# First six attention steps of a fused attention and expert kernel: own-token bonus summed on TensorE, second copy of V made on ScalarE and VectorE, new due dates for the planner

## The chip, the cores and the metric

One core of one Trainium2 chip runs the whole program. The metric is the device time of one execution in microseconds (us); of the kernel before, three timed runs are shown and one further execution that was profiled.

## The reference

The input goes through three layers. The first is a linear attention with a decaying state per head (4 sequences, 8 heads, 768 tokens, 48 values per head), in which each token also sees its own key and value through a bonus vector `u`. The second is a feed-forward layer of 384 by 2048 with a softplus. The third sends each of the 3072 tokens to one of 8 experts of 384 by 1024, by a greedy choice under a capacity of 384 tokens per expert.

```python
for t in range(S):
    cur = np.einsum('bhd,bhe->bhde', u[None] * kt, vt)
    y[:, :, t] = np.einsum('bhd,bhde->bhe', rt, state + cur)
    state = w[None, :, :, None] * state + np.einsum('bhd,bhe->bhde', kt, vt)
...
h = x @ w_in
g = np.maximum(h, 0.0) + np.log1p(np.exp(-np.abs(h)))
x = g @ w_out
...
out[mask] = np.maximum(x[mask] @ w1[e], 0.0) @ w2[e]
```

The bonus of one token and head is therefore a single number, the sum over d of r times u times k, times that token's V.

## The kernel before

**Work and stages.** Tokens go in 24 attention steps of 128 (64 tokens of two sequences) and in 8 blocks of 384 (three steps each). A step loads K, R and V (`kn`, `rn`, `vn`, two buffers each, six DMAs on SP's queue, L367) and V a second time in another layout into the lower or upper rows of `X` (two DMAs, L373), whose other rows hold the running state. VectorE scales K and R by powers of the decay (`ks`, `rs`), TensorE transposes both (L466 and L470), the results are copied to `kT` and `ar` (L351 on ScalarE, L353 on VectorE), TensorE multiplies them (`prods`, L491), VectorE masks the products (L499), TensorE forms the state's addition (`fresh`, L520) and the step's output (`outs`, L553). VectorE makes the bonus by itself: R times K (`rk`), that times `ut`, a reduction over d to `sd` (L543), and V times `sd` to `sv`, which L558 adds to the output as it leaves its bank. In the first block `tx` (L566) transposes the result into `xt`.

**Feed-forward.** Block 0 multiplies in float32: `w_in` by L673 and `w_out` by L785. Both weights arrive as 64-bit floats, in 16 chunks each (L607 and L624, four raw buffers in `third`), and VectorE makes 32-bit floats of each chunk with three instructions (L599, L601, L603). Each `w_out` chunk is also transposed (L633) and multiplied with the gate (L637). Later blocks use weights split into two 16-bit halves, which VectorE and ScalarE make (L617 and L649 the lower halves), in L678 and L788 to L790. After that come the choice of experts and the experts, which the change leaves as they are.

**What sets the order.** The program is not written in the order in which it runs. Each `op(...)` is an item with an engine, a duration, the keys it reads and writes and a due date, and `lay_out` builds every engine's list by a simulation of its own: the engine that can start first takes, among its items that could start within SLACK of each other, the one with the earliest due date. An item that names two engines goes where it would be taken first. Banks of PSUM are handed out in the same pass, and one `sp` list holds all of SP's DMAs. Once built, each engine runs its list strictly in that order and waits where something is not ready. Where TensorE's list has a gap in the simulation, `keep_warm` (L143) puts in products of a zero tile with itself, called fills below; a change to or from items marked `small` counts as a gap (SWITCH), so it gets one fill as well. Due dates come from T0, LEN and the other constants at L251 to L287: `due_att(n)` for step n, OUTLATE as a delay of the outputs from step 6 on, AHEAD as a lead of the steps over the feed-forward.

Of the kernel before, what the change touches and what calls it, by code (L numbers as in the profile page):

```python
# [9 lines left out]
FT = mybir.dt.float32  # L10
HF = mybir.dt.float16
# [3 lines left out]
OP = mybir.AluOpType  # L15
AX = mybir.AxisListType
# [5 lines left out]
def tile_kernel(ctx, tc, r, k, v, w, u, w_in, w_out, w_gate, w1, w2, out):  # L22
    nc = tc.nc
    B, H, S, D = r.shape
    DM, F = w_in.shape
# [225 lines left out]
    T0 = 15500.0  # L251
# [22 lines left out]
    AHEAD = 7500.0  # L274

    TURNED, TURN = 6, 1500.0
    HALFL = 4000.0
    HALFL2 = -4000.0
    NLAT = 6
    LATL = 400.0  # L280
    OUTLATE = 5000.0
    RAWL = 17600.0
    BITL = 14000.0
    SPLITL = -3900.0
    WOUTL = 6100.0
    ATT0 = 2600.0
    LOADL = 1600.0  # L287
# [4 lines left out]
    def several(pool, n, shape, dtype, name):  # L292
        return [pool.tile(shape, dtype, name=f"{name}{i}") for i in range(n)]
# [14 lines left out]
    XHL = several(work, 2, [128, 2 * DM], HF, "xhl")  # L308
# [30 lines left out]
    def product(o, a, b, r, w, due):  # L339
        op("dve", 470.0, lambda: DVE.tensor_mul(o, a, b), r=r, w=w, due=due)  # L340


    def scaled(eng, o, a, by):
        if eng == "act":
            ACT.mul(o, a, by)  # L345
        else:
            DVE.tensor_scalar(o, a, by, None, op0=OP.mult)

    def copied(eng, o, a):
        if eng == "act":  # L350
            ACT.copy(o, a)  # L351
        else:
            DVE.tensor_copy(o, a)  # L353
# [6 lines left out]
    def load_step(n):  # L360
        GROUP[0] = "att"
        b0, s0 = step_tok(n)
        i = n % 2
        due = due_att(n) - LOADL
        for key, src, store in (("kn", k, KN), ("rn", r, RN), ("vn", v, VN)):
            for b in range(2):
                op("sp", 650.0, lambda b=b, src=src, store=store: SP.dma_start(  # L367
                    store[i][b * 64:(b + 1) * 64], src[b0 + b, :, s0:s0 + C, :].rearrange("h s d -> s h d")),
                    w=[(key, i, b)], due=due, size=546.0)
        for q in range(2):  # L370
            src = bass.AP(tensor=v.tensor, offset=v.offset + ((b0 * H + q) * S + s0) * D,
                          ap=[[D, C], [2 * S * D, 2 * HP], [1, D]])
            op("sp", 650.0, lambda q=q, src=src: SP.dma_start(  # L373
                X[n % 3][(1 - q) * 64:(2 - q) * 64, q].rearrange("p b a d -> p (b a) d"), src),
                w=[("xv", n % 3, q)], due=due + 3.0, size=546.0)
# [15 lines left out]
                              for q in range(2)], w=["wt"], due=-1e9, size=168.0)  # L391
    op("sp", 450.0, lambda: SP.dma_start(
        ut, bass.AP(tensor=u.tensor, offset=u.offset, ap=[[0, 128], [1, H * D]])), w=["ut"], due=-500.0, size=546.0)
# [29 lines left out]

    op("dve", 3200.0, powers, r=["wt"], w=["pw", ("ar", 1, 0)], due=-1e8)
# [19 lines left out]
    def attention(n):  # L444
# [94 lines left out]


        product(rk, RN[i], KN[i], rnk + knk, ["rk"], due + 3)
        product(rk, rk, ut.rearrange("p (h d) -> p h d", h=H), ["ut"], ["rk"], due + 3)
        op("dve", 470.0, lambda: DVE.tensor_reduce(sd, rk, axis=AX.X, op=OP.add), r=["rk"], w=[("sd", i)], due=due + 3)  # L543
        product(sv, VN[i], sd[:, :, None].to_broadcast([128, H, D]), vnk + [("sd", i)], [("sv", i)], due + 3)
# [36 lines left out]
        else:  # L581
            xh, xl = XHL[i][:, :DM], XHL[i][:, DM:]
            op(FROM_SBUF, 0.0, lambda eng: scaled(eng, xh, xf, 64.0), r=[("xf", i)], w=[("xhl", i, 0)], due=due + 5)
# [9 lines left out]
    def from_double(src, t, key, due):  # L593
# [3 lines left out]
        op("sp", 450.0, lambda: src(raw), w=[("raw", c % 4)], due=due - RAWL, size=1092.0)  # L597
# [23 lines left out]
    def prep_wout(f):  # L621
# [19 lines left out]
        op("pe", 330.0, mm, r=[wt, "gate"], due=due, bank=b2)  # L641
# [751 lines left out]
    total = lay_out(items, lambda it: (it.prio, it.n), {}, True)  # L1393
# [25 lines left out]
```

## Time and profile before

| what | us |
|---|---|
| median of three runs | 778.96 (777.51 to 786.61) |
| the profiled execution's own time | 775.64 |
| its span in the trace | 773.9 |
| TensorE / VectorE / ScalarE busy in the span | 749.8 / 624.9 / 404.1 |

The span runs from the first to the last instruction; 1.74 us of the execution lie outside it. The granted TensorE clock is given as a share of the full clock (mean 0.996). TensorE's matmuls overlap in the trace, so that the time from one start to the next, not the duration, tells what one costs. A fill counts as busy.

### The profile page before, as it was taken

To read this page: it belongs to the slowest core of one execution; us is meant where nothing else is said; L and a number is where in the kernel's file an instruction comes from. 1 tells how busy PE (TensorE), PEld (TensorE's weight loads), DVE (VectorE), ACT (ScalarE), POOL (GpSimd) and SP (SyncE) were. 2 spreads that over 40 slices of the span, in tenths; PEclk is the share of its full clock that TensorE was granted. 3 is DMA by queue.
4 is the path that set the end of the run, shared out by engine and by line. 5 is a ranking of instruction groups with operands and counts; after the bars stand their busy time and mean duration, and the time that the engine had idled before them with its cause. 6 is when DMAs were issued, how large, how long until landed. Compare 5 with 4: busy or idle time off the path is not lost.

```text
span 773.9 us, 18327 instructions
## 1 busy us (share of the span) xinstructions
PE 749.8 (97%) x7202; PEld 493.0 (64%) x7202; DVE 624.9 (81%) x1711; ACT 404.1 (52%) x808; POOL 81.2 (10%) x109
## 2 busy tenths in 40 slices
PE   7999999999999999999999999999999999998996
PEld 6865677666566666667676666666666665655663
DVE  7898998999998787788999977887789879877420
ACT  2165533799766666567889911211145424436731
POOL 1000000000000000000001000000232131317731
PEclk9999999999999999999999999999999999999999
DMA  7887764412343233333110003441385664837700
GB/s 137 172 183 191 211 171 77 83 22 62 69 91 66 56 68 62 62 67 71 36 22 11 2 12 94 118 121 50 97 208 165 174 175 143 211 108 191 216 31 30
DMA packets 170901, 80.04 MB, mean 103 GB/s; under 512 B 136512, under 2 KB 166464, under 8 KB 170816
## 3 DMA queue, kind: packets, MB, share of 16 engines
q1 hardware_dynamic: 167744, 69.44, 38.3%
q0 software_dynamic: 3072, 9.44, 4.0%
q8 instruction: 56, 0.92, 0.5%
q14 instruction: 29, 0.24, 0.1%
HBM read 61.55 MB, written 9.63 MB: 92 GB/s over the span
## 4 chain that ended last, share of the span: by engine, by line
PE 67%; DVE 18%; issue 4%; ACT 4%; DMA 4%; SPq 1%; POOL 1%; POOLq 0%; ACTq 0%; DVEq 0%
PE bank L678 14%; PE bank L1292 7%; PE bank L788 7%; PE bank L789 6%; PE bank L790 6%; PE bank L785 3%; PE bank L1310 3%; PE bank L1312 3%; PE bank L1311 3%; PE bank L553 2%; PE bank L673 2%; DVE ar L499 2%; DVE gf L691 2%; PE bank L1036 2%; DMA mraw<-moe_w 1%
## 5 line engine op out<-in xcount | busy, mean ns | idle before, releaser
L678 PEld LDWEIGHTS <-wi 128*128 128x128 f16 x1008 | 97.3, 98 | 65.2 <-issue 2.0
L678 PE MATMUL bank<-xt,wi 128*128 128x384 f16 x672 | 127.6, 326 | 0.0
L684 ACT ACTIVATE ta<-bank 128x384 f32<-128x384 f32 x128 | 61.5, 482 | 43.3 <-PE bank L678 30.2
L789 PE MATMUL bank<-wo,g 128*128 128x384 f16 (+1 forms) x240 | 78.4, 327 | 0.9 <-DVE wo L649 0.7
L788 PE MATMUL bank<-wo,g 128*128 128x384 f16 (+1 forms) x240 | 78.5, 327 | 0.0
L790 PE MATMUL bank<-wo,g 128*128 128x384 f16 (+1 forms) x240 | 78.5, 327 | 0.0
L691 DVE SCALAR_TENSOR_TENSOR gf<-bank,ta 128x384 f32<-128x384 f32 x112 | 61.8, 553 | 17.2 <-ACT ta L686 16.0
L678 PE MATMUL bank<-xs,wi 128*128 128x384 f16 x336 | 72.9, 326 | 0.0
L1292 PE MATMUL bank<-g,w1h 128*128 128x384 f16 x384 | 72.9, 326 | 0.0
L685 ACT ACTIVATE ta<-ta 128x384 f32<-128x384 f32 x128 | 66.5, 522 | 2.9
L686 ACT ACTIVATE ta<-ta 128x384 f32<-128x384 f32 x128 | 66.2, 519 | 2.5
L1312 PE MATMUL bank<-w2h,g 128*128 128x384 f16 x192 | 62.6, 326 | 0.0
L1310 PE MATMUL bank<-w2h,g 128*128 128x384 f16 x192 | 62.6, 326 | 0.0
L1311 PE MATMUL bank<-w2l,g 128*128 128x384 f16 x192 | 62.5, 326 | 0.0
L1296 ACT ACTIVATE g<-bank 128x384 f16<-128x384 f32 x64 | 30.7, 489 | 40.4 <-PE bank L1292 24.7
L1292 PEld LDWEIGHTS <-w1h 128*128 128x128 f16 x384 | 35.8, 98 | 22.6 <-issue 0.4
L1299 DVE SCALAR_TENSOR_TENSOR g<-bank,g 128x384 f16<-128x384 f32 x64 | 34.1, 548 | 19.4 <-ACT g L1296 19.3
L698 DVE SCALAR_TENSOR_TENSOR g<-gf,g 128x384 f16<-128x384 f32 x80 | 44.0, 553 | 3.1 <-ACT g L345 1.8
L499 DVE TENSOR_TENSOR ar<-bank,mask 64x256 f32<-64x256 f32 x96 | 40.5, 422 | 4.6 <-PE bank L491 2.3
L345 ACT ACTIVATE x2o<-bank 128x384 f16<-128x384 f32 x19 | 9.3, 490 | 65.3 <-PE bank L790 39.2
L1205 POOL DMA_INDIRECT third<-x2d,idx x24 | 25.8, 1074 | 155.7 <-DVE db L1009 130.0
L1292 PE MATMUL bank<-g,w1l 128*128 128x384 f16 x192 | 41.7, 326 | 0.0
(227 smaller groups left out, 1533.3 us busy)
## 6 DMA issues: line engine op xcount, KB each, us to landing
mraw<-moe_w SPq DMA_DIRECT2D x64, 384.0 KB, 4.0
third<-moe_w_in SPq DMA_DIRECT2D x16, 384.0 KB, 5.0
third<-moe_w_out SPq DMA_DIRECT2D x16, 384.0 KB, 3.5
kn<-k SPq DMA_DIRECT2D x48, 96.0 KB, 3.1
rn<-r SPq DMA_DIRECT2D x48, 96.0 KB, 3.1
vn<-v SPq DMA_DIRECT2D x48, 96.0 KB, 3.0
X<-v SPq DMA_DIRECT2D x48, 96.0 KB, 3.1
x2d<-x2o SPq DMA_DIRECT2D x48, 96.0 KB, 2.2
```

The costliest lines, as they stand in the source:

```text
L678: PE.matmul(ph, WF[:, f, a, kk, :], x[:, kk, :], start=(i == 0), stop=(i == 3 * KC - 1))
L684: op("act", 371.0, lambda: ACT.activation(ta, bank.view(BT), AF.Abs), w=[("ta", c)], due=due, bank=bank)
L685: op("act", 413.0, lambda: ACT.activation(ta, ta, AF.Exp, scale=-1.0), w=[("ta", c)], due=due)
L686: op("act", 413.0, lambda: ACT.activation(ta, ta, AF.Ln, bias=1.0), w=[("ta", c)], due=due)
L691: op("dve", 470.0, lambda: DVE.scalar_tensor_tensor(gf, bank.view(BT), 0.0, ta, op0=OP.max, op1=OP.add), r=[("ta", c)], w=[("gf", c)], due ...
L788: PE.matmul(p, gh[:, f, ts], WU[:, f, 0, :no], start=(f == 0), stop=False)
L789: PE.matmul(p, gh[:, f, ts], WU[:, f, 1, :no], start=False, stop=False)
L790: PE.matmul(p, gl[:, f, ts], WU[:, f, 0, :no], start=False, stop=(f == FC - 1))
L1292: PE.matmul(ph, a[:, kk, fs], XH[p][:, x0 + kk, :], start=(i == 0), stop=(i == 3 * KC - 1))
L1310: PE.matmul(po, h1h[:, f, js], w2h[:, fz, :], start=(f == 0), stop=False)
L1311: PE.matmul(po, h1h[:, f, js], w2l[:, fz, :], start=False, stop=False)
L1312: PE.matmul(po, h1l[:, f, js], w2h[:, fz, :], start=False, stop=(f == FB - 1))
```

## The change

For the first six steps the bonus is made in another way: VectorE multiplies the transposed R, still in its bank, with `kT` (one product of 128 by 512, called `rkT`, which lies in the memory of `xhl`), TensorE multiplies each head pair's part of it with a table `uw` of two columns that holds u times the decay (`sums`, four float32 matmuls of two columns), and VectorE multiplies V with these sums from their bank. `uw` comes from `uq`, two further small DMAs. The second copy of V is made in the first six steps from `vn`, in four copies of 64 by 192 by ScalarE or VectorE, in place of the two DMAs; V itself and everything from step 6 on stay. Several constants of due dates, DMA sizes and one duration of the planner are new, and the simulation's clocks of SP and VectorE start at 1000 and 900.

```diff
-    T0 = 15500.0
+    T0 = 16250.0
...
-    AHEAD = 7500.0
+    AHEAD = 10500.0
...
+    COPIED = 6
...
-    OUTLATE = 5000.0
+    OUTLATE = 8750.0
...
-    XHL = several(work, 2, [128, 2 * DM], HF, "xhl")
+    XHL2 = work.tile([128, 2, 2 * DM], HF, name="xhl")
+    XHL = [XHL2[:, i] for i in range(2)]
...
+        if n < COPIED:
+            for q in range(2):
+                for b in range(2):
+                    op({"act": 260.0, "dve": 180.0}, 0.0, lambda eng, q=q, b=b: copied(
+                        eng, X[n % 3][(1 - q) * 64:(2 - q) * 64, q, b],
+                        VN[i][b * 64:(b + 1) * 64].rearrange("p (a q) d -> p a q d", q=2)[:, :, q, :]),
+                        r=[("vn", i, b)], w=[("xv", n % 3, q)], due=due_att(n) + 2.5)
+            return
...
+    op("sp", 1300.0, lambda: [SP.dma_start(uq[q * 64:q * 64 + D], u.rearrange("(p q) d -> q d p", q=2)[q])
+                              for q in range(2)], w=["uq"], due=-1000.0, size=168.0)
     op("sp", 450.0, lambda: SP.dma_start(
-        ut, bass.AP(tensor=u.tensor, offset=u.offset, ap=[[0, 128], [1, H * D]])), w=["ut"], due=-500.0, size=546.0)
+        ut, bass.AP(tensor=u.tensor, offset=u.offset, ap=[[0, 128], [1, H * D]])), w=["ut"], due=due_att(3), size=1200.0)
...
+    def factors():
+        DVE.memset(uw, 0.0)
+        for q in range(2):
+            DVE.tensor_mul(uw[q * 64:q * 64 + D, :, q], uq[q * 64:q * 64 + D], wt[q * 64:q * 64 + D])
+
+    op("dve", 300.0, factors, r=["wt", "uq"], w=["uw"], due=2.5)
...
+        if n < TURNED:
+            op("dve", 602.0, lambda: DVE.tensor_tensor(rkT, b2.view(HP, 128), kT, op=OP.mult), r=[("kT", i)], w=["rkT"],
+               due=due + 3, bank=b2)
+
+            def sums():
+                for pr in range(HP):
+                    PE.matmul(b7.view(H)[:, 2 * pr:2 * pr + 2], rkT[:, pr, :], uw[:, pr, :], start=True, stop=True)
+
+            b7 = Bank("att")
+            op("pe", 900.0, sums, r=["rkT", "uw"], w=[("sd", i)], due=due + 3, bank=b7)
+            op("dve", 470.0, lambda: DVE.tensor_tensor(sv, VN[i], b7.view(H)[:, :, None].to_broadcast([128, H, D]), op=OP.mult),
+               r=vnk, w=[("sv", i)], due=due + 3, bank=b7)
+        else:
+            bonus()
...
-        op("pe", 330.0, mm, r=[wt, "gate"], due=due, bank=b2)
+        op("pe", 670.0, mm, r=[wt, "gate"], due=due, bank=b2)
...
-    total = lay_out(items, lambda it: (it.prio, it.n), {}, True)
+    total = lay_out(items, lambda it: (it.prio, it.n), {"sp": 1000.0, "dve": 900.0}, True)
```

The first place is the head of SP's list. In the kernel before, a chunk of `w_in`, the second copy of V (`X0`), `ut` and another chunk stand ahead of step 1's K (`kn1`):

```order
L390 DMA wt_139<-w 48x4x1 x2
L607 DMA third_131<-moe_w_in 128x3x256
L367 DMA kn0_93<-k 64x8x48 x2
L367 DMA rn0_91<-r 64x8x48 x2
L367 DMA vn0_95<-v 64x8x48 x2
L373 DMA X0_97<-v 64x8x48 x2
L392 DMA ut_140<-u 128x384
L607 DMA third_131<-moe_w_in 128x3x256
L367 DMA kn1_94<-k 64x8x48 x2
```

In the change it reads (`uq` is the small table of u):

```order
L400 DMA wt_138<-w 48x4x1 x2
L369 DMA kn0_93<-k 64x8x48 x2
L369 DMA rn0_91<-r 64x8x48 x2
L369 DMA vn0_95<-v 64x8x48 x2
L369 DMA kn1_94<-k 64x8x48 x2
L369 DMA rn1_92<-r 64x8x48 x2
L369 DMA vn1_96<-v 64x8x48 x2
L646 DMA third_130<-moe_w_in 128x3x256
L402 DMA uq_149<-u 48x4x1 x2
```

Five transfers that stood ahead of step 1's K are gone from there: two of `w_in`, two of `X0` and `ut`.

The second place is VectorE's list in step 2 (the third), from R times K on, in the kernel before:

```order
L340 TENSOR_TENSOR rk0_104<-rn0_91,kn0_93 128x384
L599 TENSOR_SCALAR wi_134<-third_131 128x384
L340 TENSOR_TENSOR rk0_104<-rk0_104,ut_140 128x384
L353 COPY ar0_111<-bank5_85 64x8x64
L527 TENSOR_TENSOR wx0_113<-bank6_86,wx0_113 128x4x48
L527 TENSOR_TENSOR wx0_113<-bank1_81,wx0_113 128x4x48
L543 TENSOR_REDUCE sd0_105<-rk0_104 128x8
L499 TENSOR_TENSOR ar0_111<-bank0_80,mask_144 64x4x64 x2
L499 TENSOR_TENSOR ar0_111<-bank2_82,mask_144 64x4x64 x2
L340 TENSOR_TENSOR wx0_113<-wx0_113,sq_145 128x384
L340 TENSOR_TENSOR sv0_107<-vn0_95,sd0_105 128x384
```

The same step in the change, from the copy to `ar` on:

```order
L355 COPY ar0_111<-bank5_85 64x8x64
L571 TENSOR_TENSOR xhl_116<-bank5_85,kT0_109 128x512
L640 SCALAR_TENSOR_TENSOR wi_133<-third_130,wi_133 128x384
L355 COPY X2_99<-vn0_95 64x192
L522 TENSOR_TENSOR ar0_111<-bank0_80,mask_143 64x4x64 x2
L355 COPY X2_99<-vn0_95 64x192
L522 TENSOR_TENSOR ar0_111<-bank1_81,mask_143 64x4x64 x2
L550 TENSOR_TENSOR wx0_113<-bank6_86,wx0_113 128x4x48
L550 TENSOR_TENSOR wx0_113<-bank4_84,wx0_113 128x4x48
L580 TENSOR_TENSOR sv0_107<-vn0_95,bank3_83 128x384
L342 TENSOR_TENSOR wx0_113<-wx0_113,sq_144 128x384
```

Two products and the reduction have become one product of 512 columns, and two of the four copies of V stand on VectorE here (the other two on ScalarE).

The third place is TensorE's list in a late block (the outputs of step 12). Before, `outs` stands by itself, behind a fill of its own and ahead of the feed-forward's next products:

```order
L790 MATMUL bank_82<-wo,g_130 128x392
L143 LDWEIGHTS still
L143 MATMUL bank_87<-still 128x128
L553 MATMUL bank_84<-X_97,ar_111 64x48 x16
L788 LDWEIGHTS g_129
L788 MATMUL bank_82<-wo,g_129 128x392
```

In the change it stands behind the next step's transposes, and its own step's `fresh` (L543, 16 matmuls of which the first is shown) and the next step's `prods` follow on it:

```order
L829 MATMUL bank_86<-wo,g_129 128x392
L489 MATMUL bank_85<-identf,ks_103 128x128 x4
L493 MATMUL bank_84<-identf,rs_101 128x128 x4
L143 LDWEIGHTS still
L143 MATMUL bank_87<-still 128x128
L592 MATMUL bank_81<-X_97,ar_111 64x48 x16
L543 MATMUL bank_82<-vn_95,ks_102 64x48
```

The outputs have moved back beside the next step's products, and one fill serves the three groups of small products.

## Rows read from the trace of the kernel before

**Rows 1.** Busy time by stretch: stretch, length, each engine's busy time, clock, DMA
```profile
6.58:37.83 31.25, 26.95 (x517) 23.70 (x517) 25.52 (x59) 7.06 (x13) 0.00 (x0) 0.95 0.83 167
...
39.00:86.06 47.06, 44.81 (x355) 28.93 (x356) 44.03 (x104) 26.71 (x56) 0.00 (x0) 1.00 0.79 193
86.06:142.10 56.04, 56.04 (x698) 40.89 (x698) 51.07 (x120) 22.96 (x57) 0.00 (x0) 1.00 0.60 137
142.10:173.80 31.70, 31.41 (x226) 19.03 (x225) 31.17 (x76) 29.37 (x70) 0.82 (x2) 1.00 0.22 42
```

**Rows 2.** The chain of waits in order of time: start us, us, what
```profile
39.00 4.14 PE bank L673 x12
44.82 1.95 PE bank L673 x6
55.73 3.95 DMA third<-moe_w_in
...
81.36 1.50 PE bank L637 x12
...
203.01 1.46 PE bank L678 x9
...
210.02 1.07 PE bank L553 x32
```

**Rows 3.** Timeline of VectorE before 38 us: start, us, instruction, idle before
```profile
12.56 0.56 DVE L340 TENSOR_TENSOR rk<-rk,ut 128x384 f32<-128x384 f32 x1 [1.85 <-DMA ut<-u]
...
16.59 0.56 DVE L340 TENSOR_TENSOR ks<-kn,pwn 128x384 f32<-128x384 f32 x1 [1.26 <-DMA kn<-k]
...
30.66 0.55 DVE L340 TENSOR_TENSOR rk<-rn,kn 128x384 f32<-128x384 f32 x1
31.13 0.35 DVE L599 TENSOR_SCALAR wi<-third 128x384 int32<-128x384 int32 x1
31.40 0.55 DVE L340 TENSOR_TENSOR rk<-rk,ut 128x384 f32<-128x384 f32 x1
32.17 0.69 DVE L353 COPY ar<-bank 64x512 f32<-64x512 f32 x1 [0.23 <-ACT ar L351]
...
33.44 0.54 DVE L543 TENSOR_REDUCE sd<-rk 128x8 f32<-128x384 f32 x1
...
36.30 0.55 DVE L340 TENSOR_TENSOR sv<-vn,sd 128x384 f32<-128x384 f32 x1
36.88 0.36 DVE L353 COPY X<-wx 64x384 f32<-64x384 f32 x1
37.27 0.56 DVE L558 TENSOR_TENSOR xf<-bank,sv 128x384 f32<-128x384 f32 x1
```

**Rows 4.** Timeline of SP's queue: start, us to issue, what
```profile
6.60 1.31 SPq L373 DMA_DIRECT2D X<-v  x2
7.96 0.62 SPq L392 DMA_DIRECT2D ut<-u  x1
...
9.10 1.29 SPq L367 DMA_DIRECT2D kn<-k  x2
```

**Rows 5.** Timeline of TensorE in the first block and in a late one
```profile
62.46 0.66 PE L466 MATMUL bank<-identf,ks 128*128 128x128 f32 x4 [1.56 <-DVE ks L340]
...
275.14 0.60 PE L466 MATMUL bank<-identf,ks 128*128 128x128 f32 x4
275.57 0.60 PE L470 MATMUL bank<-identf,rs 128*128 128x128 f32 x4
...
278.47 0.22 PE L143 MATMUL bank<-still 128*128 128x128 bf16 x1
278.62 0.69 PE L491 MATMUL bank<-ar,kT 64*64 64x64 f32 x32
279.13 0.63 PE L520 MATMUL bank<-vn,ks 64*64 64x48 f32 x32
279.70 0.34 PE L788 MATMUL bank<-wo,third 128*128 128x392 f16 x1
```

More of the change, by code (lines that the diff above doesn't have):

```diff
@@ L368, in load_step @@
                     store[i][b * 64:(b + 1) * 64], src[b0 + b, :, s0:s0 + C, :].rearrange("h s d -> s h d")),
-                    w=[(key, i, b)], due=due, size=546.0)
+                    w=[(key, i, b)], due=due, size=640.0)
+        if n < COPIED:
[6 more added lines that the diff above has]
+            return
         for q in range(2):
@@ L374, in load_step @@
                 X[n % 3][(1 - q) * 64:(2 - q) * 64, q].rearrange("p b a d -> p (b a) d"), src),
-                w=[("xv", n % 3, q)], due=due + 3.0, size=546.0)
+                w=[("xv", n % 3, q)], due=due + 3.0, size=640.0)
     wt = const.tile([128, HP], FT, name="wt")
@@ L538, in attention, with bonus @@
                    r=[("wx", 0), ("wx", 1)], w=[("st", y, q)], due=due + 3)
[L541 to L544, printed above, removed]
+        def bonus():
+            product(rk, RN[i], KN[i], rnk + knk, ["rk"], due + 3)
+            product(rk, rk, ut.rearrange("p (h d) -> p h d", h=H), ["ut"], ["rk"], due + 3)
+            op("dve", 470.0, lambda: DVE.tensor_reduce(sd, rk, axis=AX.X, op=OP.add), r=["rk"], w=[("sd", i)], due=due + 3)
+            product(sv, VN[i], sd[:, :, None].to_broadcast([128, H, D]), vnk + [("sd", i)], [("sv", i)], due + 3)
+        if n < TURNED:
[10 more added lines that the diff above has]
+            bonus()
         b5, b6 = Bank("att"), Bank("att")
@@ L582, in attention @@
             xh, xl = XHL[i][:, :DM], XHL[i][:, DM:]
-            op(FROM_SBUF, 0.0, lambda eng: scaled(eng, xh, xf, 64.0), r=[("xf", i)], w=[("xhl", i, 0)], due=due + 5)
+            op(FROM_SBUF, 0.0, lambda eng: scaled(eng, xh, xf, 64.0), r=[("xf", i)], w=[("xhl", i, 0), "rkT"], due=due + 5)
             op("dve", 470.0, lambda: DVE.scalar_tensor_tensor(xl, xf, 64.0, xh, op0=OP.mult, op1=OP.subtract),
@@ L596, in from_double @@
         raw = RAW[c % 4]
-        op("sp", 450.0, lambda: src(raw), w=[("raw", c % 4)], due=due - RAWL, size=1092.0)
+        op("sp", 450.0, lambda: src(raw), w=[("raw", c % 4)], due=due - RAWL, size=1900.0)
         hi, lo = [raw[..., i] if len(t.shape) == 2 else raw[..., i].rearrange("p (k f) -> p k f", k=KC) for i in (1, 0)]
```

13 lines of the change are left out of this document (8 added, 5 removed).

## Prediction

> **What bounds the kernel now.** I read the busy times by stretch first. From 39 us on TensorE hardly stops: 44.8 of 47.1 us, 56.0 of 56.0, 31.4 of 31.7 [rows 1]. So what the change is worth there is what TensorE's own list gets shorter by, and the waits hidden in it. Before 39 us TensorE also looks busy, but most of it is fills: the built list has 258 of them ahead of the first L673. That matmul starts at 39.00 [rows 2], because block 0 multiplies all three steps of its tokens at once and step 2's output leaves VectorE at 37.27 [rows 3]. The head is thus a chain through VectorE, which worked 25.52 of the 31.25 us from 6.58 to 37.83 [rows 1] and stood still for 5.73. Of that stillness, 1.85 was a wait for `ut` and 1.26 one for step 1's K [rows 3], whose load SP issued only at 9.10, behind X, `ut` and two chunks of `w_in` [rows 4].
>
> After 39 us, waits still hide inside the overlapping matmuls, so I set the list against the clock. From 39.0 to 173.8 (134.8 us) it holds 96 float32 matmuls of 384 or 392 columns at 0.65 (three, two records each, took 1.95), 16 gate products at 0.75 (two took 1.50), 15 groups of L678 at 1.46, seven `outs` at 1.07 [rows 2], 15 transposes of K or R at 0.43, eight `fresh` at 0.57 and seven `prods` at 0.51 [rows 5], and 16 transposes of `w_out` and three of the output, three quarters of a K transpose each, 0.33. That is 62.4 + 12.0 + 21.9 + 7.5 + 6.5 + 4.6 + 3.6 + 6.3 = 124.8. The other 10.0 us are fills, changes to small matmuls, and waits for VectorE and for weights; the clearest is 1.56 us at 62.46 [rows 5], behind a chunk of `w_in` that the chain waits 3.95 for [rows 2].
>
> **The head.** VectorE loses, per step, R times K, times `ut`, V times `sd` (each 0.47 from start to start, 30.66 to 31.13) and the reduction, 0.57 from 33.44 to 34.01 [rows 3]: 1.98, and 5.9 in three steps. It gains the product of 512 columns from a bank. No row shows one; the nearest below is 0.55, a product of 384 columns, and above it twice that; the copy of 512 columns from a bank takes 0.69 [rows 3], which I take. V times the sums, with one operand in a bank, is priced like `xf`, 0.5. That is 1.2 per step, 3.6 in three. In VectorE's list up to step 2's output there are also two conversion instructions (0.47 each) and one 0.27 scale fewer, together 1.2, and four half copies of V more at about half of 0.36, less one copy of the state, and three small instructions for `uw`: +0.9. Work: 25.5 - 5.9 + 3.6 - 1.2 + 0.9 = 22.9.
>
> Of the stillness the wait for `ut` goes (it is first used in step 6). The wait for K goes too: SP now issues it after two small DMAs and six loads, by 0.65 each (two took 1.31 [rows 4]) about 3.3 us earlier, with no `w_in`, X or `ut` in front of it on the DMA engines, which were 0.83 busy [rows 1]. Something must be late next: the copies of V wait for `vn`, and `uw` for `uq`, two DMAs issued at about 10.3 that VectorE needs after step 0's masks, near 16; step 1's K, issued from 9.10 on, was there at 16.59 [rows 3, 4], and `uq`, as slow as that, would be 1 to 2 us late. I keep the other 2.6 us of stillness. Step 2's output then ends at 6.58 + 22.9 + 2.6 = 32.1 in place of 37.83, and block 0 starts **5.7 us earlier**, near 33.3. Bounds: 3 if new waits take as much as K's and `ut`'s did, 7.5 if half of the kept stillness goes as well. ScalarE's share of the V copies costs nothing: it works 7.06 of 31.25 us there [rows 1], and TensorE's fills cover the three `sums`. Without that cover each copy, at most the 0.51 that a copy of twice the size takes, would be 1 us per step.
>
> **After the head.** Each `sums` is four float32 matmuls with 128 columns of weights, two passes each. The trace has no matmul of two columns. The nearest is the gate product of eight columns: 12 passes in 1.50 us [rows 2], 0.125 a pass; so eight passes take 1.0 us, and three of the six `sums` come after the start of block 0: **+3.0**. Bounds: 0.8 in all if a pass ran as fast as one of `outs` (32 in 1.07), 4.5 if half a group's length again were lost at each change of form.
>
> The Trainium skill's page TensorE: Matmul & The Clock Gate (section Wait — 56ns, not 53.3ns?) gives about 25 ns from start to start as the floor for however few columns. By that the three `sums` would take 3 x 8 x 0.025 = 0.6 and the whole change would win 2.4 us more; the row of the eight-column product disagrees, five times as long, and decides.
>
> The list after block 0's start has 50 fills or runs of fills up to the choice of experts in the kernel before and 40 in the change, since `outs` now stands beside the next step's products. One costs 0.15 (278.47 to 278.62) [rows 5]: **-1.5** (bounds 0 and -2). Of the waits, the change should remove the 1.56 us behind a late chunk of `w_in`: twelve 96 KB transfers leave the first six steps, 1.2 MB, or about 6 us of the 193 GB/s that moved there [rows 1]. I take **-1.6** (bounds +5 and -6 for all waits of the 10 us together, since the order is another). All other due dates only permute work on a TensorE that is full: nothing.
>
> **Sum**, against the profiled execution's 775.64: -5.7 + 3.0 - 1.5 - 1.6 = -5.8, which is 769.8. The median of the runs shown lies 3.3 above that execution, so I predict 773.0.
>
> **Rivals.** *A, VectorE is the bound in the first two blocks, and the result is slower.* For: it works 44.0 of 47.1, 51.1 of 56.0 and 31.2 of 31.7 us after 39 [rows 1], and the new due dates put more in front of the last `w_out` conversion. Counting its list by the spacings above, 95 us of work lie between step 2's output and that conversion, against 81 before. From 32.1 it would end at 127 without one pause, and TensorE comes to it near 33.3 + 95 = 128. So the margin is 1 us; from there each pause costs the same on TensorE. Waiting for `sums` is such a pause: they stand in TensorE's list behind or beside an L673 group of 1.95, and masks and conversions are queued behind `sv`. At 1.95 for each of three steps, other pauses of 3.0 as in the stretch from 39 to 86, less the margin of 1, and none of the 1.6 saved, the sum is -5.7 + 3.0 - 1.5 + 5.9 + 3.0 - 1.0 = +3.7: 779.3 by the profile, 782.7 by the median. Against: in VectorE's list some nine instructions stand between `rkT` and `sv`.
>
> *B, the head's gain is lost again, but no more.* The waits grow by about as much as the start comes earlier: TensorE waits for VectorE's conversions by 4 to 6 us, 774 to 776 by the profile, 778 by the median.
>
> *C, the waits go.* VectorE's steps get shorter by 0.8 and the DMAs fewer, and of the 10 us between list and clock 5 more go, the start gains 7: 763.5 by the profile, 767 by the median. For: the list keeps steps further ahead of their use. Against: rival A's margin.
>
> *D, the sums are as cheap as the smallest rows*: -2.2 more, 771; it stays inside the forecast's own range.
>
> **How the numbers follow.** Forecast (768 to 776.5): 0.55, rival D in it. B: 0.18. C: 0.17. A: 0.10. From 765.5 up to 780 about 2 in 10 is left out, the better part of A and the low end of C. About 2%, 15.6 us, is what a measurement of this kernel can tell from no change: a gain of that size needs C and more (0.04), a loss of it more than A's price (0.02).
>
> **What the profile of the changed kernel would show.** The first L712 (the former L673) near 33 rather than 39; no VectorE wait for `ut` or for step 1's K; `sums` near 1.0 us from start to the next matmul; the first L827 (formerly L788 at 173.8) near 169 to 171, and the choice of experts 5 to 7 us earlier, with the part after it as long as now. I am wrong about the head if the first L712 is after 36; about TensorE's list if the stretch from there to the first L827 is longer than 138 us, which would be A or B with conversions or `sv` named as what TensorE waits for; about the sums if they take 0.3.

## The result and the profile after

The changed kernel takes 770.21 us (median of four runs, 769.70 to 771.63) beside 778.24 for the kernel before (median of four), a ratio of 0.9874 with a 95% interval from 0.9833 to 0.9915: faster by 1.3%, and less than the 2% by which a difference counts here. (The two medians alone give 0.990, inside the interval.) The profiled execution took 769.70, 5.9 less than that of before. The prediction was 773.0 (765.5 to 780.0), and 769.8 for the profiled execution. The total is right; some of its terms are not, and what they miss nearly cancels.

The page's busy times and chain, by engine, after the change:

```profile
span 767.6 us, 18281 instructions
...
PE 750.8 (98%) x7160; PEld 491.6 (64%) x7160; DVE 621.8 (81%) x1718; ACT 403.4 (53%) x816; POOL 80.2 (10%) x109
...
PE 73%; DVE 16%; issue 4%; DMA 3%; ACT 2%; SPq 1%; POOL 1%; POOLq 0%; DVEq 0%; ACTq 0%
```

TensorE is busy 1 us more (749.8 before) and the span is 6.3 shorter: what went was time in which TensorE stood still, 24.1 us before and 16.8 now. The stretches that answer to [rows 1] (columns as there: stretch, length, busy time of TensorE's products (PE), its weight loads (PEld), VectorE (DVE), ScalarE (ACT) and GpSimd (POOL), granted clock, DMA share, GB/s), and the long stretch behind them:

```profile
6.58:32.19 25.61, 23.99 (x467) 21.08 (x467) 22.70 (x55) 10.33 (x23) 0.00 (x0) 1.00 0.86 179
33.36:86.00 52.64, 52.40 (x575) 36.61 (x576) 51.19 (x121) 38.35 (x84) 0.00 (x0) 1.00 0.73 179
86.00:137.20 51.20, 50.73 (x487) 34.69 (x486) 49.30 (x114) 19.85 (x50) 0.00 (x0) 1.00 0.75 155
137.20:172.80 35.60, 35.59 (x281) 21.52 (x280) 35.38 (x88) 32.53 (x78) 0.82 (x2) 1.00 0.13 26
172.80:447.50 274.70, 274.13 (x3070) 180.73 (x3069) 234.17 (x578) 190.77 (x401) 1.93 (x9) 1.00 0.26 51
```

The head's 31.25 us are 25.61 now; VectorE works 22.70 of them (25.52 before) and stands still for 2.91 (5.73). Its timeline, the rows that answer to [rows 3]:

```profile
7.80 0.43 DVE L451 COPY kT<-ar 128x512 f32<-128x512 f32 x1 [0.75 <-PE bank L457]
...
10.13 0.55 DVE L342 TENSOR_TENSOR ks<-kn,pwn 128x384 f32<-128x384 f32 x1
...
11.79 0.69 DVE L355 COPY ar<-bank 64x512 f32<-64x512 f32 x1 [0.56 <-ACT ar L353]
...
16.02 0.35 DVE L444 TENSOR_TENSOR uw<-uq,wt 48x4 f32<-48x4 f32 x2
...
26.71 0.69 DVE L571 TENSOR_TENSOR xhl<-bank,kT 128x512 f32<-128x512 f32 x1
...
31.64 0.55 DVE L597 TENSOR_TENSOR xf<-bank,sv 128x384 f32<-128x384 f32 x1
```

Step 1's `ks` starts at 10.13 and waits for nothing (16.59 after a wait of 1.26 before), `uw` finds `uq` there, and the product `rkT` (printed with the tile it lies in, `xhl`) takes 0.69. SP issues step 1's K at 6.11 instead of 9.10 [rows 4]:

```profile
6.11 1.31 SPq L369 DMA_DIRECT2D kn<-k  x2
...
10.84 2.24 SPq L402 DMA_DIRECT2D uq<-u  x2
```

The late K probably cost the kernel before more than the 1.26 us. Two stretches of its head, and VectorE's row that falls into the second:

```profile
14.00:18.00 4.00, 2.06 (x44) 1.81 (x45) 2.63 (x6) 0.19 (x1) 0.00 (x0) 0.93 0.50 83
18.00:22.00 4.00, 4.00 (x81) 3.63 (x79) 3.18 (x9) 0.59 (x1) 0.00 (x0) 0.64 0.99 217
```

```profile
20.67 0.62 DVE L527 TENSOR_TENSOR wx<-bank,wx 128x192 f32<-128x192 f32 x2 [0.65 <-PE bank L520]
```

TensorE stood still for half of the first stretch, its clock was 0.64 in the second, and there VectorE waited 0.65 for it. In the change the clock is 1.00 through the whole head (0.95 before).

TensorE's timeline shows the new sums and the start of block 0 (39.00 in [rows 2]):

```profile
16.67 1.05 PE L576 MATMUL bank<-uw,xhl 128*128 128x2 f32 x8
17.59 0.63 PE L493 MATMUL bank<-identf,rs 128*128 128x128 f32 x4
...
33.36 0.91 PE L712 MATMUL bank<-xt,wi 128*128 128x384 f32 x2
```

From start to next start a group of sums takes 0.92.

All kernels of this study stand against the same four marks, read from the first starts of four lines: block 0 (L712), the first later-block product with `w_out` (L827), the first count of the choice of experts (L1075), the first product of the experts (L1331). "Work" is TensorE's list between the first two marks by the prices of the prediction (sums at 0.92, in e6 at 2.70); "rest" is what the clock shows beyond it. "Later" runs from the second mark to the first count.

| kernel | block 0 at | to first L827 | work | rest | later | count to experts | experts | ratio to before (95%) |
|---|---|---|---|---|---|---|---|---|
| before | 39.0 | 134.8 | 124.8 | 10.0 | 282.1 | 101.9 | 216.1 | 1 |
| the change | 33.4 | 139.5 | 131.4 | 8.1 | 274.6 | 102.5 | 217.6 | 0.9874 (0.9833 to 0.9915) |
| e1 dates alone | 36.0 | 129.3 | 114.9 | 14.4 | 288.0 | 104.8 | 218.5 | 0.9961 (0.9931 to 0.9990) |
| e2 forms alone | 34.6 | 135.2 | 119.8 | 15.4 | 288.5 | 101.9 | 216.8 | 1.0023 (0.9998 to 1.0048) |
| e3 no copies | 35.2 | 137.7 | 124.1 | 13.6 | 284.0 | 104.0 | 216.0 | 1.0009 (0.9985 to 1.0034) |
| e4 no sums | 33.4 | 142.6 | 128.6 | 14.0 | 274.6 | 102.4 | 217.6 | 0.9943 (0.9912 to 0.9974) |
| e5 old lead | 33.4 | 138.6 | 130.0 | 8.6 | 278.1 | 102.9 | 215.9 | 0.9900 (0.9874 to 0.9926) |
| e6 sums thrice | 41.8 | 143.5 | 136.7 | 6.8 | 275.9 | 102.5 | 216.7 | 1.0082 (1.0051 to 1.0113) |
| e8 loads ahead | 38.7 | 139.6 | 131.4 | 8.2 | 274.7 | 102.3 | 217.7 | 0.9966 (0.9945 to 0.9986) |
| e10 no fills | 33.5 | 139.2 | 131.4 | 7.8 | 274.6 | 101.8 | 217.5 | 0.9865 (0.9839 to 0.9892) |
| e11 no sums, short fills | 33.6 | 142.5 | 128.6 | 13.9 | 274.4 | 102.2 | 215.1 | 0.9915 (0.9893 to 0.9938) |
| e12 loads added | 35.7 | 144.3 | 131.4 | 12.9 | 274.4 | 103.2 | 217.8 | 0.9953 (0.9926 to 0.9981) |
| e13 copies on ScalarE | 33.3 | 141.8 | 131.4 | 10.4 | 275.2 | 102.0 | 217.5 | 0.9915 (0.9881 to 0.9949) |

(e9, the kernel e3 with short fills, has a ratio of 0.9998, 0.9968 to 1.0028; its profiled execution took 789.6 us, 9 more than its median, so its stretches are not used.)

So where did the 6.3 us of span go? Block 0 starts 5.6 earlier. From there to the first L827 the clock shows 4.7 more, but the list holds 6.6 more: three groups of sums (2.76), two L717 groups more (2.92), one transpose of R and one `prods` (0.94); the rest fell from 10.0 to 8.1. The later part is 7.5 shorter, 3.9 of it that moved work, 3.6 fewer waits. And 2.1 were given back behind the first count (0.6 and 1.5), where the instructions are the same in all these kernels (but for one product in e1) and the same two stretches range from 101.8 to 104.8 and from 215.1 to 218.5 by themselves: I take that part for scatter between executions, though with one trace of each kernel that is not shown.

### The profile page after: what moved, and what is told of

It is laid out like the page before. It is cut to its first block, busy times and chain, and to the rows that moved or that the text cites. A ratio compares the mean times of both kernels' runs of the same rounds, so it can differ in the third digit from the quotient of the medians.

```text
span 767.6 us, 18281 instructions
## 1 busy us (share of the span) xinstructions
PE 750.8 (98%) x7160; PEld 491.6 (64%) x7160; DVE 621.8 (81%) x1718; ACT 403.4 (53%) x816; POOL 80.2 (10%) x109
## 4 chain that ended last, share of the span: by engine, by line
PE 73%; DVE 16%; issue 4%; DMA 3%; ACT 2%; SPq 1%; POOL 1%; POOLq 0%; DVEq 0%; ACTq 0%
PE bank L717 18%; PE bank L1331 7%; PE bank L827 7%; PE bank L829 6%; PE bank L828 6%; PE bank L824 4%; PE bank L1349 3%; PE bank L1350 3%; PE bank L1351 3%; PE bank L1075 2%; PE bank L592 2%; DVE ar L522 2%; PE bank L676 1%; PE bank L514 1%; PE bank L543 1%
## 5 line engine op out<-in xcount | busy, mean ns | idle before, releaser
L717 PEld LDWEIGHTS <-wi 128*128 128x128 f16 x1008 | 96.8, 98 | 65.8 <-issue 2.1
L717 PE MATMUL bank<-xt,wi 128*128 128x384 f16 x672 | 127.6, 326 | 0.0
L827 PE MATMUL bank<-wo,g 128*128 128x384 f16 (+1 forms) x240 | 78.5, 327 | 0.0
L717 PE MATMUL bank<-xs,wi 128*128 128x384 f16 x336 | 72.9, 326 | 0.0
L1331 PE MATMUL bank<-g,w1h 128*128 128x384 f16 x384 | 72.9, 326 | 0.0
L1335 ACT ACTIVATE g<-bank 128x384 f16<-128x384 f32 x64 | 30.7, 488 | 41.8 <-PE bank L1331 26.0
L1331 PEld LDWEIGHTS <-w1h 128*128 128x128 f16 x384 | 35.8, 98 | 24.0 <-issue 2.0
L347 ACT ACTIVATE x2o<-bank 128x384 f16<-128x384 f32 x23 | 11.1, 485 | 64.3 <-PE bank L829 37.6
L1331 PE MATMUL bank<-g,w1l 128*128 128x384 f16 x192 | 41.7, 326 | 0.0
```

Of the source, the lines that this page charges most:

```text
L717: PE.matmul(ph, WF[:, f, a, kk, :], x[:, kk, :], start=(i == 0), stop=(i == 3 * KC - 1))
L827: PE.matmul(p, gh[:, f, ts], WU[:, f, 0, :no], start=(f == 0), stop=False)
L1331: PE.matmul(ph, a[:, kk, fs], XH[p][:, x0 + kk, :], start=(i == 0), stop=(i == 3 * KC - 1))
```

## The experiments

**The parts apart.** My theory was that the head gains from less work on VectorE and from earlier loads together, and that the copies of V are a minor part; the rival, that the due dates make the gain.

```diff
# e1: the kernel before, with
-    T0 = 15500.0
+    T0 = 16250.0
...
-        ut, bass.AP(tensor=u.tensor, offset=u.offset, ap=[[0, 128], [1, H * D]])), w=["ut"], due=-500.0, size=546.0)
+        ut, bass.AP(tensor=u.tensor, offset=u.offset, ap=[[0, 128], [1, H * D]])), w=["ut"], due=-2000.0, size=1200.0)
# e2: the change, with
-    T0 = 16250.0
+    T0 = 15500.0
...
# e3: the change, with
-    COPIED = 6
+    COPIED = 0
# e4: the change, with
-        if n < TURNED:
+        if n < SUMMED:
...
+    SUMMED = 0
```

(e1 and e2 exchange all eight due dates, the sizes, the one duration and the start clocks; e4 changes the condition of the bonus alone, leaves out `uq` and `uw`, and loads `ut` as e1 does.)

> The kernel before with the new due dates, sizes and start clocks only (bonus on VectorE, second copy of V by DMA; ut is loaded right behind X of step 0, ahead of step 1's K). My theory: the first block's start needs both less VectorE work (2.6 us) and earlier loads. Here only the loads can help (two chunks of w_in no longer stand ahead of step 1's K), VectorE's 25.5 us stay, so block 0 starts at 36 to 38 instead of 39.0; no sums, so TensorE's list after it is 2.8 us shorter than in the change. Profiled time 771 to 774 against 775.64 before and 769.7 for the change. Rival (the due dates make the gain, the new forms are neutral): block 0 starts at 33 to 34 and the time is 767 to 770.

> The change with the due dates, sizes and start clocks of the kernel before. My theory: VectorE's work in the head is 22.9 us and ut is gone from it, but one chunk of w_in and uq stand ahead of step 1's K, so block 0 starts at 34 to 36; the outputs are not merged with the next step's products (50 runs of fills against 43 after the head), so about 1 us of the later gain is missing: profiled time 770 to 773. Rival (dates alone): block 0 starts at 38 to 39, time 775 to 778, since the sums add 2.8 to TensorE's list.

> The change with the second copy of V by DMA again in all steps (twelve transfers of 96 KB more in the first six steps, 24 copies of 64x192 less). My theory: the copies of V are a minor part; they take about 0.5 us per step of VectorE in the head, the DMAs cost 1.3 us of SP per step ahead of the next step's K. Block 0 starts at 33 to 35; waits for w_in come back by up to 1.6 us after it; profiled time 769 to 772. Rival (the freed loads make the gain): block 0 starts after 36 and the time is 773 to 776.

> The change with the bonus by VectorE again in all steps (ut loaded behind step 0's V; no uq, uw, rkT, sums). My theory: VectorE gets 0.8 us more per step, 2.3 in the head, so block 0 starts at 35.5 to 36.5; TensorE's list after that is 2.8 us shorter, but VectorE (97% busy there) gives back 1 to 2 of these: profiled time 769 to 772, within 1.5 us of the change. Rival 1 (VectorE's work is not the head's bound): block 0 starts at 33.4 and the time is 767. Rival 2 (VectorE bounds the first two blocks too): the stretch from block 0's start to the first L827-like matmul is as long as in the change or longer, time 773 to 775.

Measured: block 0 at 36.0, 34.6, 35.2 and 33.4; ratios 0.9961, 1.0023, 1.0009 and 0.9943. Neither theory stands, and the times of e1, e2 and e3 (778.4, 778.7 and 778.7 profiled; e1's median is 775.2) lie beyond every range that was expected. The dates alone bring 3.0 us in the head and the forms alone 4.4, as mine said, but both then lose them on the way to the first L827, where the rest is 14 to 15 us instead of 8. The copies of V are no minor part: without them all of the gain is gone. And e4 takes my reason for the head away: with the bonus back on VectorE block 0 starts at 33.4 all the same, as its first rival had it, while the stretch behind it is longer, as its second had it. Two stretches of e4, the head up to step 2's output and from block 0 to the first L827:

```profile
6.58:32.27 25.69, 24.28 (x494) 21.02 (x494) 23.49 (x54) 10.62 (x23) 0.00 (x0) 1.00 0.84 186
33.40:176.00 142.60, 141.31 (x1380) 94.45 (x1380) 139.42 (x329) 92.14 (x215) 0.82 (x2) 1.00 0.56 128
```

In the head VectorE works 23.49, only 0.8 more than in the change: the bonus takes 6.5 there against 3.7, but the planner puts three conversion instructions ahead of step 2's output instead of six (1.2 less) and one copy to `ar` fewer (0.7), `uw` is not made (0.4), and the stillness is 2.2 instead of 2.9. The conversions left over are due in the next stretch, where VectorE now works 139.4 of 142.6, 3.5 more than in the change. It is 3.1 longer than in the change although TensorE's list is 2.8 shorter. So the sums pay behind the start of block 0 and not in the head; e4's lists are planned anew, so the 3.1 us are those of the whole new order.

In e3 the same stretch shows who is late. Waits of the weight loads (line, waited for, us in total, times, longest), first of e3, then of the change:

```profile
PEld bank L676 <- ACT third L353: 5.1, 10, 0.6
PEld bank L672 <- DVE wo L642: 4.2, 8, 1.0
PEld bank L712 <- DVE wi L642: 1.7, 2, 1.2
```

```profile
PEld bank L676 <- ACT third L353: 6.3, 11, 0.6
...
PEld bank L672 <- DVE wo L642: 1.1, 1, 1.1
```

The transposes of `w_out` (L672) wait eight times for VectorE's conversions (L642) instead of once, and block 0's products twice for those of `w_in`. Whether that comes from the loads or from the other order that the planner makes once it counts them is open here; e8 and e12 take it up.

**The fills.** e3 and e4 also hold more fills than the change between block 0's start and the first L827: 72 and 80 against 17. e10 takes all 40 out of the change; e9 and e11 cut the runs of e3 and e4 to one.

```diff
             k = int((it.start - last - 100.0) / step)
+            if BEGIN[0].start < it.start < COUNT[0].start:
+                k = min(k, 0)
```

(`BEGIN` and `COUNT` hold the first items of L712 and L1075; e9 and e11 have 1 in place of 0.)

> The kernel without copies of V (second copy by DMA in all steps, as measured before: ratio 1.0009, block 0 from 35.2, then 137.7 to the first later-block w_out product with 13.0 us beside 124.7 of work), and every run of fills behind block 0's start cut to one fill, 51 fills fewer. Theory F (the planner puts fills where it believes that TensorE waits for weights, and on a full TensorE each costs its 0.06 us): the stretch falls by 51 times 0.062 = 3 us to 134.5, time 774 to 775. Theory W (TensorE really waits there for conversions of late weights, and the fills lie in these waits): the stretch stays at 137 to 138 and the time at 776 to 778.

> The change without any fill from block 0's start to the first count (40 fills in 40 runs fewer); the order of all else is that of the change. The prediction priced a fill at 0.15 us on a full TensorE. By that price the time falls by 40 times 0.15 = 6 us: 763 to 765 profiled, ratio near 0.980. Rival (a switch to or from the small products costs that time with or without a fill, so the fills lie in it): 769 to 770, ratio as that of the change, 0.987. Between them, a fill at the 0.06 us of a fill in a row: -2.4, 767.

> The kernel without sums (bonus by VectorE in all steps, as measured before: ratio 0.9943, block 0 from 33.4, then 142.6 to the first later-block w_out product for 129.2 of work), and every run of fills behind block 0's start cut to one fill, 55 fills fewer. Theory F (the long runs of fills cost TensorE): the stretch falls by 55 times 0.062 = 3.4 to 139, time 767 to 768, better than the change. Theory V (VectorE, busy 139.4 of the 142.6, is what bounds the stretch without the sums, and the fills lie in waits for it): the stretch stays at 142 to 143 and the time at 770 to 771.

Measured: ratios 0.9998 (e3: 1.0009), 0.9865 (the change: 0.9874) and 0.9915 (e4: 0.9943), each inside the other's interval or overlapping it, and the stretches to the first L827 139.2 against 139.5 (the later part is 274.6 in both) and 142.5 against 142.6. Forty fills less give back 0.3 us, not 6; e9, for which only times count, has a median of 780.5 and so is not the 774 to 775 of its theory F. Fills cost nothing worth naming. The rows of TensorE show why; first step 12's outputs in the change, then the same place without its fill (K's and R's transposes, outputs, additions to the state; lines three higher):

```profile
280.04 0.60 PE L493 MATMUL bank<-identf,rs 128*128 128x128 f32 x4
280.47 0.22 PE L143 MATMUL bank<-still 128*128 128x128 bf16 x1
280.62 1.14 PE L592 MATMUL bank<-X,ar 128*64 128x48 f32 x32
```

```profile
279.52 0.60 PE L496 MATMUL bank<-identf,rs 128*128 128x128 f32 x4
...
280.05 1.14 PE L595 MATMUL bank<-X,ar 128*64 128x48 f32 x32
281.12 0.68 PE L546 MATMUL bank<-vn,ks 64*64 64x48 f32 x32
```

From the transposes to the outputs it is 0.58 with the fill and 0.53 without: the change of form takes that time, and the fill lies in it but for 0.05. In e11 TensorE's busy time falls by 2.8 us against e4 (138.47 for 141.31) and the stretch by 0.1; the long runs of fills had lain in waits. That leaves VectorE, which works 139.4 us of the stretch in both and waits 1.3 in e4, as the likely bound of e4 and e11 there.

**The lead of the outputs.** e5 takes OUTLATE and AHEAD back; up to the third block the change's lists stay.

```diff
-    AHEAD = 10500.0
+    AHEAD = 7500.0
...
-    OUTLATE = 8750.0
+    OUTLATE = 5000.0
```

> The change with AHEAD and OUTLATE of the kernel before; up to the third block all lists are those of the change, from there the outputs stand by themselves again, with five more runs of fills. My theory: the part from the first later-block w_out product to the first count took 274.6 in the change for 258.5 of work, 16.1 of rest, against 282.0 for 262.4, 19.6 of rest, before; so the old lead gives 2 to 3.5 back there (less 0.5 because one step's transposes and products stand behind the mark instead of ahead of it), head and first two blocks as in the change (33.4 and about 138): 772 to 774 profiled, ratio 0.989 to 0.994. Rival (the late order is worth nothing; the gain behind the mark comes from what the first blocks leave it): within 1 us of the change.

Measured: the later part takes 278.1 instead of 274.6, with 1.4 us more work behind the mark, so 2.1 more waits there, and 0.5 more ahead of it; the first count comes at 450.1 instead of 447.5. The ratio, 0.9900, stands beside 0.9874 with intervals that overlap. The change, e4, e6, e8, e10, e11 and e12, whose products in the later part are the same, lie there between 274.4 and 275.9, so 278.1 is clear of them: the stretches say what the medians alone could not. The two constants were not tried apart.

**The loads.** e8 puts two chunks of `w_in` and `ut` ahead of step 1's K in SP's list and leaves every other engine's list as it is; the traces show the same instructions in the same order on all of them, in e12 as well. e12 leaves all in place and adds the twelve transfers that the copies of V had replaced, into memory that nothing uses yet.

```diff
# e8
-        for _, _, it in sorted(order, key=lambda z: z[:2]):
+        for _, _, it in sorted(order, key=lambda z: (K1[0].start, -1) if z[2] in HEAD else z[:2]):
# e12
             it.fn()
+            for at, load in EXTRA:
+                if at is it:
+                    load()
```

> The change with SP's list alone in another order: two chunks of w_in (393 KB each) and ut stand ahead of step 1's K, as in the kernel before; every other engine's list is that of the change. Theory L (the early loads make the head's gain): step 1's K, used at 10.13 in the change, lands 3 to 5 us later, VectorE waits there, block 0 starts at 35.5 to 38 and the time is 772 to 774. Theory W (VectorE's shorter list makes it, waits are caught up later): block 0 starts at 33.4 to 34.5, time 769 to 771.

> The change with twelve transfers more: the second copy of V is still made from the first, and beside that loaded behind each step's V of the first six steps into memory that is used by nothing before 137 us. All engine lists but SP's are those of the change. Theory T (the transfers themselves cost, in SP's time of 0.65 each and in bytes, 1.2 MB): block 0 starts at 34.5 to 36, weights come later and the next 139.5 get 3 to 5 longer: 774 to 777, most of what the kernel without the copies lost (ratio 1.0009). Theory O (that kernel lost by the other order that the planner makes of its belief about the loads): block 0 at 33.4 to 34, time 769 to 771.

Measured for e8: block 0 at 38.7, all but 0.3 of the head's gain gone, and everything behind it as in the change (139.6, 274.7). This is the plainest result of the study: undoing the order of SP's list alone undoes the head. Theory L holds, with a loss above its range (38.7 and 775.1 for 35.5 to 38 and 772 to 774). VectorE's wait for step 1's K and the next one for TensorE, and four stretches around them:

```profile
14.27 0.56 DVE L343 TENSOR_TENSOR ks<-kn,pwn 128x384 f32<-128x384 f32 x1 [3.95 <-DMA kn<-k]
...
18.56 1.78 DVE L526 TENSOR_TENSOR ar<-bank,mask 64x256 f32<-64x256 f32 x4 [1.38 <-PE bank L518]
```

```profile
12.00:16.00 4.00, 1.02 (x6) 0.99 (x7) 1.70 (x4) 0.51 (x1) 0.00 (x0) 0.73 0.73 99
16.00:20.00 4.00, 4.00 (x86) 3.71 (x85) 2.48 (x7) 1.98 (x5) 0.00 (x0) 0.50 0.74 152
20.00:24.00 4.00, 4.00 (x67) 3.83 (x66) 3.53 (x11) 0.38 (x1) 0.00 (x0) 0.92 0.71 197
24.00:28.00 4.00, 3.84 (x75) 3.49 (x72) 3.79 (x9) 2.11 (x5) 0.00 (x0) 1.00 0.46 106
```

VectorE waits 3.95 us, and the loss is 5.3: TensorE stands still with it (busy 1.02 of 4) and then runs at the lower of its two levels, 1.2 GHz, from 16 to 20 (clock 0.50), where VectorE waits 1.38 for TensorE in turn.

Measured for e12: block 0 at 35.7, 2.3 later, and the way to the first L827 144.3, 4.8 longer at the same list; ratio 0.9953. The transfers themselves cost, then. VectorE's waits for DMAs say how:

```profile
11.37 0.56 DVE L346 TENSOR_TENSOR ks<-kn,pwn 128x384 f32<-128x384 f32 x1 [1.17 <-DMA kn<-k]
...
18.40 0.36 DVE L453 TENSOR_TENSOR uw<-uq,wt 48x4 f32<-48x4 f32 x2 [1.69 <-DMA uq<-u]
...
47.06 0.36 DVE L647 TENSOR_SCALAR wi<-third 128x384 int32<-128x384 int32 x1 [2.36 <-DMA third<-moe_w_in]
```

Each SP entry ahead of a load costs it 0.65 or more (SP issues step 1's K at 7.47 instead of 6.11 and `uq` at 14.51 instead of 10.84), so both are late, and one chunk of `w_in` holds VectorE for 2.36 us. Behind that wait TensorE has gaps and its clock falls; three stretches, then two of its rows, the first at the lower level, the second later at the upper one (L721 is the change's L712; x6 is three float32 products, two records each):

```profile
44.00:48.00 4.00, 3.38 (x32) 2.21 (x25) 1.55 (x5) 2.95 (x7) 0.00 (x0) 1.00 0.99 311
48.00:52.00 4.00, 2.99 (x48) 2.53 (x52) 3.84 (x9) 0.85 (x2) 0.00 (x0) 0.71 1.24 196
52.00:56.00 4.00, 4.00 (x31) 2.39 (x27) 3.54 (x9) 0.00 (x0) 0.00 (x0) 0.50 0.87 199
```

```profile
52.58 4.13 PE L721 MATMUL bank<-xt,wi 128*128 128x384 f32 x6
...
61.62 2.10 PE L721 MATMUL bank<-xt,wi 128*128 128x384 f32 x6
```

TensorE's gaps from 44 to 52 are 1.6 us, and the lower clock takes another 3.4 (4 us at 0.71, 4 at 0.50, 4 at 0.94, the last from the next stretch): together 5.0, beside the 4.8 by which the stretch is longer. This profiled execution, at 777.5, is 2.9 above the median of e12's runs (774.6), so the fall of the clock need not be as long in each.

**What the sums cost.** e6 multiplies every group three times into the same columns.

```diff
-                for pr in range(HP):
+                for pr in [*range(HP), *range(HP), *range(HP)]:
```

> The change with every group of sums multiplied three times in a row into the same columns (24 passes in place of 8), all orders as in the change. A group took 0.92 us, so each gets 1.84 longer. Theory P (TensorE's list bounds the first two blocks): three of the six groups stand there, the stretch from block 0's start to the first later-block w_out product goes from 139.5 to 145.0, and the head is later by up to 1 where VectorE waits for the sums: time 775 to 777, ratio 0.994 to 0.997. Theory V (VectorE, busy 135.9 of the 139.5, bounds it as much): part of the 5.5 is hidden, the stretch is 140 to 143, time 770 to 774.

Measured: 2.70 a group instead of 0.92, so 5.3 more in three groups behind block 0's start; the stretch is 4.0 longer. Most of TensorE's added work shows, some 1.3 lie in what had been waits. That is nearer to theory P, but both missed the head: block 0 starts at 41.8, 8.4 later. TensorE's rows and three stretches of the head:

```profile
33.48 2.84 PE L576 MATMUL bank<-uw,xhl 128*128 128x2 f32 x24
36.18 0.22 PE L143 MATMUL bank<-still 128*128 128x128 bf16 x1
```

```profile
20.00:24.00 4.00, 4.00 (x63) 3.61 (x62) 3.45 (x7) 1.61 (x3) 0.00 (x0) 0.59 0.75 163
...
28.00:32.00 4.00, 4.00 (x51) 3.90 (x50) 1.81 (x5) 1.19 (x3) 0.00 (x0) 0.63 0.53 113
...
36.00:40.00 4.00, 4.00 (x85) 3.68 (x86) 2.67 (x8) 0.51 (x1) 0.00 (x0) 0.73 0.05 9
```

The three groups of the head add 5.3 to TensorE's list. Behind them VectorE waits 7.4 us, in the change 0.4: 1.90 and 2.05 at `sv` behind the first two groups, 0.90 for the `fresh` behind the third, and 2.6 at three other places. From step 2's output to block 0 it is 1.1 longer as well. In the three stretches the clock was 0.59, 0.63 and 0.73 although TensorE counted as busy throughout; in the change it is 1.00 there. How much of the 8.4 is the clock and how much the longer groups, the run does not tell. So the sums' place in the head is not free for any length: at 0.92 TensorE's slack covers them, at 2.70 it does not.

**A variant.** e13 puts the last four copies of V on ScalarE as well.

```diff
-                    op({"act": 260.0, "dve": 180.0}, 0.0, lambda eng, q=q, b=b: copied(
-                        eng, X[n % 3][(1 - q) * 64:(2 - q) * 64, q, b],
+                    op("act", 260.0, lambda q=q, b=b: copied(
+                        "act", X[n % 3][(1 - q) * 64:(2 - q) * 64, q, b],
```

> The change with all 24 copies of V on ScalarE (20 before, 4 on VectorE, all four in the head, 1.26 us with the gaps). If VectorE's list sets the head, block 0 starts near 32.4 and the time is 768 to 769; if not, 33.4 and 769 to 771. It could be better than the change by at most 1.3 us; within the intervals, no difference, is the likeliest.

Measured: block 0 at 33.3, ratio 0.9915, no better. The copies' 1.26 us are gone from VectorE's head, but the planner put a conversion more into their place, and the stretch to the first L827 is 2.3 longer, with four waits of L672 for conversions (3.4 us) in place of one (1.1). Of the versions tried none beats the change by more than the runs differ; e10's 0.9865 is the same time.

## Why the prediction was right, and where it was not

**The head, -5.7: the size held, the reason half.** Measured: -5.6; work of VectorE 22.70 (predicted 22.9), stillness 2.91 (2.6), no wait for `ut` or K, step 2's output at 32.19 (32.1). Two of the counts in 22.9 are off by one and nearly cancel: by the traces one conversion fewer stands ahead of step 2's output, not two, and two copies of the state fewer, not one. The kept 2.6 us of stillness held as a sum, not wait by wait: 0.65 for TensorE went, with the clock of 0.64, and waits of 0.75 and 0.56 are new. But "less work on VectorE" and "earlier loads" were added as if each were worth its own time. By e8 undoing the loads' order alone takes back 5.3 of the 5.6; by e4 the bonus may return to VectorE and nothing happens to the start of block 0, since the planner then moves three conversions behind it and a copy to ScalarE. The step that failed is the reading of VectorE's 25.5 us as a fixed list: part of it is work of the next stretch that the planner uses as filling. The guess that `uq` would come 1 to 2 us late was wrong in the change (no wait) and came true, at 1.69, in e12 with its added loads.

**The three sums, +3.0: the price held, the sign of the edit did not.** A group takes 0.92 (predicted 1.0, from the gate product's passes); the floor of 25 ns that the Trainium skill's page TensorE: Matmul & The Clock Gate (section Wait — 56ns, not 53.3ns?) gives makes an estimate of 0.2. That is a least time and no price: the trace has 0.115 a pass, and TensorE's weight loads, one for each pass, are busy for 0.97 us of a group:

```profile
16.67 0.97 PEld L576 LDWEIGHTS bank<-uw,xhl 128*128 128x128 f32 x8
```

e6 confirms that what is added there is mostly paid, 4.0 of 5.3. But the sum had no term for what the sums relieve: without them (e4) the same stretch is 3.1 longer, with 3.5 more work on VectorE, which at 97% of the stretch is as full as TensorE. This was in rows 1 (44.0 of 47.1, 51.1 of 56.0 and 31.2 of 31.7) and was used in rival A alone, as a danger. Rival A itself did not come: VectorE's listed waits on the way to the first L827 are 1.7 us in all, none of them for sums.

**Switches and fills, -1.5: wrong.** The 0.15 was the distance from a fill to the next product; taken out, a fill gives back 0.05 or less (e10), and ten fewer are worth nothing. What the merged outputs and the longer lead are worth together is in the waits and changes of form, 2.6 by e5, where the prediction said that all other due dates do nothing.

**The wait behind `w_in`, -1.6: right as far as the traces show.** In the change VectorE waits for no chunk from block 0 to the first L827, where it waited 2.4 us once before, and the rest fell by 1.9 (10.0 to 8.1). VectorE's waits there (line, waited for, us in total, times, longest), first of the kernel before, its longest alone, then all of the change:

```profile
DVE wi L599 <- DMA third<-moe_w_in: 2.4, 1, 2.4
```

```profile
DVE ar L355 <- ACT ar L353: 1.0, 2, 0.7
DVE kT L355 <- PE bank L489: 0.4, 1, 0.4
DVE wo L688 <- ACT wo L347: 0.3, 1, 0.3
```

In e12 the twelve transfers bring back a wait of 2.36, and with the clock that falls behind it 4.8 us; in the profiled execution of the kernel before the clock stayed at 1.00 behind its wait [rows 1], so that further price does not belong to this term. What had no term at all are the 3.6 us of waits that went in the later part.

**The sum.** Behind block 0's start the prediction had -0.1 (+3.0 - 1.5 - 1.6). Up to the first count the traces show -2.8: +2.8 for the sums and -5.6 for waits, near rival C. Then 2.1 were lost again in the part that the change leaves as it is, which no step foresaw, and 0.4 more lie outside the span (2.1 for 1.7). With the head that is -5.6 - 2.8 + 2.1 + 0.4 = -5.9. That 769.8 met 769.7 is luck: fills priced at 1.5 that are worth nothing, 3.6 of waits that were not foreseen, and 2.5 lost elsewhere. For the median I had carried over that the shown median of before lies 3.3 above its profiled execution; the change's profiled execution lies 0.5 below its own median, and the 2.8 between them are the miss of 773.0 against 770.2. The medians of four differ by 8.0 where the profiles differ by 5.9.

**One test was badly made.** The stretch from block 0 to the first L827 was to show a false TensorE list if longer than 138 us; it took 139.5 (the first L827 came at 172.9 for 169 to 171, the choice of experts 8.4 us earlier for 5 to 7). The mark had moved: two L717 groups and a step's products that stood behind it before stand ahead of it now. Set against its own list, the stretch has 8.1 of rest, less than the 10.0 before.

**What stays open.** The parts pay little alone: dates, forms, copies or sums taken away (e2, e1, e3, e4) raise the rest between block 0 and the first L827 by 5 to 7 us, and the old order of the loads (e8) moves the head by 5. For the loads (e8, e12) the cause is shown, with all other lists unchanged. For VectorE's bonus (e4, e11) the numbers fit, but the planner made new lists. For e1 and e2 the cause was not tried apart; e2's stretch also holds a clock of 0.97, about 3.4 us. Of e3's loss the transfers alone (e12) give 0.0079 of 0.0135 in the ratio; whether the remainder is the planner's other order was not tried.

## What to carry to other kernels

Where a planner fills an engine's pauses with later work, the engine's busy time ahead of a mark is no fixed cost: ask which of it could stand behind the mark, and look at the order of the loads first. When two engines are both full in a stretch, moving work from one to the other is worth what it frees there, and must not be booked as a cost of the receiver alone. And a stretch is compared against its own list of work: a mark that is passed by other work moves without any time being gained or lost.

## What the runs showed of the hardware

A wait of TensorE can be paid twice. In e8 it was busy 1.02 of 4 us, and the next 4 us had a granted clock of 0.50; in the kernel before it was busy 2.06 of 4 us, and 0.64 followed; in e12 gaps of 1.6 us lay beside clocks of 0.71 and then 0.50, and three float32 products of 384 columns took 3.96 from start to start where they take 1.93 at the upper level. The Trainium skill's page TensorE: Matmul & The Clock Gate (section HAM oscillation — how this bites in real kernels) tells the same of a kernel in which every wait for a load was followed by products at the lower clock; the trace of e8 agrees.

The clock also fell in e6, to 0.59, 0.63 and 0.73, while TensorE counted as busy without a gap, behind groups of 24 passes of two columns; with eight passes, in the change, it stayed at 1.00. In these rows a full busy share stands beside a low clock, so the two columns are read together.

At the place shown, a fill between two forms of products took 0.05 us, though it stands in the timeline with 0.22 and with 0.15 to the next start; forty of them were worth 0.3 us.
